# Scaling and DMA transposes of each batch placed in the order of their loads, in a retention-plus-MLP kernel

## The chip, the cores and the metric

The kernel runs on one core of a Trainium2 chip. The metric is the device time of one execution in microseconds (us). The record marks a run as slow when it lies over 1.5% above the fastest of its kernel.

The engines in the views: PE is TensorE (matmul), PEld its weight loads, DVE is VectorE, ACT ScalarE, POOL GpSimd, SP SyncE. A "q" behind an engine (SPq, ACTq) is its queue, in which it issues DMAs.

## The reference

Eight batches of eight heads, 576 tokens of width 64, go through a retention layer; the result (4608 tokens of width 512) goes through an MLP with a Swish whose slope is an input. All is float32 in memory.

```python
scores = scale * np.matmul(q, k.transpose(0, 1, 3, 2))
ret = scores * Dmat[None]                    # gamma_h ** (i - j) where i >= j, else 0
x = np.matmul(ret, v)                        # then heads side by side: [4608, 512]
h = x @ w_in                                 # [4608, 2048]
g = h / (1.0 + np.exp(-beta * h))
return g @ w_out                             # [4608, 512]
```

## The kernel before

The kernel is one long, hand-ordered program. TensorE's bulk is the MLP, cut into *fill steps* of four 512-column matmuls; block m computes the MLP of batch m while the attention of the next batch is slipped between its steps. All other work hangs on a number: the fill step before which it is put into the program of its engine. Each engine works strictly in that order.

```python
def merged(fill, *streams):
    todo = sorted((x for st in streams for x in st), key=lambda x: x[0])
    for n, f in enumerate(fill):
        while todo and todo[0][0] <= n:
            todo.pop(0)[1]()
        f()
```

A batch of attention is four chunks of 128 tokens; each pair of batches has a *tail* for the 64 tokens left over of both. A chunk needs these stages, each on another engine:

```python
# load_q, load_kv, load_tail: SyncE issues the loads
# pre_q(b, n), pre(i):        POOL scales queries and values, casts keys to bf16
# x_q, x_k, x_tail:           ScalarE issues a DMA that transposes
# a_sc, a_O, a_st:            TensorE: scores, output, state
def turn(dst, src):
    nc.scalar.dma_start_transpose(dst.rearrange("p j pr s -> p (j pr) s"), src.rearrange("p j h d -> p (j h d)"))
```

The distances between these stages are the numbers in question. Chunk `(b, c)` is computed at step `at`:

```python
def group(i, at):
    ...
    if b is None:                                              # a tail
        st += [(at - 27, F(load_tail, c)), (at - 15, F(pre, i)), (at - 10, F(x_tail, i))]
    else:
        near = b == 2
        if c == 0:
            xs, ps = ((10, 8), (15, 14, 13, 12)) if near else ((13.5, 12), (19, 18, 17, 16))
            st += [(at - 31, F(load_q, b))] + [(at - a, F(pre_q, b, x)) for x, a in enumerate(ps)]
            st += [(at - a, F(x_q, b, x)) for x, a in enumerate(xs)]
        if c % 2 == 0:                                         # keys and values, by pairs of chunks
            p0, p1, x0 = (9, 8.5, 5) if near else (15, 14.5, 10.5)
            st += [(at - 28, F(load_kv, n)), (at - 27.5, F(load_kv, n + 1)), (at - p0, F(pre, i)),
                   (at - p1, F(pre, i + 1)), (at - x0, F(x_k, b, c // 2))]
```

Batches 0 and 1 are transposed on TensorE instead, with a copy on ScalarE or VectorE behind it.

## Time and profile before

| | us |
|---|---|
| time, median of 3 runs at first | 326.29 |
| the same beside the changed kernel, 4 runs | 326.19 (325.56 to 327.77) |
| span of the profiled execution | 324.1 |
| TensorE busy | 303.4 (94%) |
| PE waits for transposed keys | 8.9 in two waits |
| batch 3's first scores start at | 96.79 |

The span and the busy times by engine are the head of the profile's page:

```profile
span 324.1 us, 5208 instructions
...
PE 303.4 (94%) x2078; PEld 153.2 (47%) x2113; DVE 109.7 (34%) x191; ACT 135.1 (42%) x236; POOL 103.8 (32%) x132
```

A share of 94% leaves about 20 us in which PE isn't busy, and some busy time that is stretched by a low clock. The share doesn't say which of these 20 us can be won. That takes the slices, the waits of PE and the chain of waits, which the prediction shows and reads.

### The profile page before, as it was taken

How to read it: one execution, taken by the hardware profiler on the slowest of the kernel's cores; microseconds unless marked ns; L12 is line 12 of the kernel's file. 1: busy time of each engine (PE TensorE's matmuls, PEld its weight loads, DVE VectorE, ACT ScalarE, POOL GpSimd, SP SyncE). 2: the span in 40 equal slices, each digit the busy share in tenths (PEclk: the TensorE clock that was granted, in tenths of full speed). 3: DMA queues.
4: the chain of work that ended last, by engine and by line, in shares of the span. 5: the costliest groups of instructions: out<-in, count | busy, mean ns of one | idle time of the engine just before them, and what ended most of it. 6: DMA issues, size and time to landing. Idle time of an engine off the chain costs nothing.

```text
span 324.1 us, 5208 instructions
## 1 busy us (share of the span) xinstructions
PE 303.4 (94%) x2078; PEld 153.2 (47%) x2113; DVE 109.7 (34%) x191; ACT 135.1 (42%) x236; POOL 103.8 (32%) x132
## 2 busy tenths in 40 slices
PE   6779989986499999999999999999999999999996
PEld 4544446432245444544454445444544544444444
DVE  6745665013245213522452246103622520020012
ACT  5567336560104740374027502750276107505800
POOL 2653785606820382138228210283310000000000
PEclk9799999999699999999999999999999999999999
DMA  8999999999916999499989643999711100022002
GB/s 203 242 359 386 369 215 265 194 266 236 220 68 172 206 213 189 133 207 198 243 227 197 106 122 99 224 212 221 185 39 32 62 37 32 2 66 65 2 38 92
DMA packets 127592, 53.83 MB, mean 166 GB/s; under 512 B 109888, under 2 KB 119504, under 8 KB 127568
## 3 DMA queue, kind: packets, MB, share of 16 engines
q1 hardware_dynamic: 97968, 46.15, 60.2%
q10 hardware_dynamic: 29600, 7.35, 14.2%
q8 instruction: 16, 0.26, 0.4%
q14 instruction: 8, 0.07, 0.1%
HBM read 36.71 MB, written 9.44 MB: 142 GB/s over the span
## 4 chain that ended last, share of the span: by engine, by line
PE 83%; DMA 8%; SPq 4%; issue 1%; DVE 1%; POOL 1%; ACT 0%
PE po L405 37%; PE ph L392 35%; PE O L350 3%; PE sc L312 3%; SPq L91 3%; DMA wt<-in_moe_w_in_dram 2%; DMA kvn<-in_v_dram 2%; PE O L336 2%; DMA qT<-qs 2%; PE st L375 2%; DMA kT<-kn 2%; SPq L80 1%; DVE ot L412 1%; PE O L333 0%; POOL kn L265 0%
## 5 line engine op out<-in xcount | busy, mean ns | idle before, releaser
L392 PE MATMUL ph<-xT,w_in_sb 128*128 128x512 bf16 (+2 forms) x577 | 127.4, 373 | 2.5 <-ACT w_in_sb L178 1.3
L405 PE MATMUL po<-w_out_sb,gT 128*128 128x512 bf16 (+2 forms) x588 | 127.9, 370 | 1.0
L394 ACT ACTIVATE gT<-ph,beta_sb 128x512 bf16<-128x512 f32 (+2 forms) x148 | 98.5, 675 | 62.0 <-PE ph L392 58.9
L392 PEld LDWEIGHTS <-w_in_sb 128*128 128x128 bf16 x592 | 56.4, 98 | 65.8 <-ACT w_in_sb L178 1.7
L405 PEld LDWEIGHTS <-gT 128*128 128x128 bf16 x608 | 57.6, 98 | 62.2 <-issue 1.4
L317 DVE TENSOR_TENSOR R<-sc,causal 128x512 bf16<-128x512 f32 x72 | 46.3, 684 | 82.8 <-PE sc L312 82.8
L412 DVE COPY ot<-po 128x512 f32<-128x512 f32 (+2 forms) x38 | 25.2, 663 | 113.5 <-PE po L405 112.3
L242 POOL TENSOR_TENSOR qs<-qn,gq 128x512 bf16<-128x512 f32 x26 | 27.0, 1061 | 62.9 <-DMA qn<-in_q_dram 48.9
L266 POOL TENSOR_TENSOR vn<-kvn,gv 128x512 bf16<-128x512 f32 x32 | 33.3, 1042 | 25.9 <-PE st L375 12.4
L380 ACT CAST sbd<-st 64x256 bf16<-64x256 f32 x48 | 17.6, 366 | 52.8 <-PE st L375 34.8
L265 POOL CAST kn<-kvn 128x512 bf16<-128x512 f32 x32 | 19.5, 609 | 22.5 <-DMA kT<-kn 7.1
L312 PE MATMUL sc<-qT,kT 64*128 64x128 bf16 x256 | 13.3, 224 | 10.0 <-DMA kT<-kn 8.9
L380 ACT CAST end<-st 64x256 bf16<-64x256 f32 x16 | 5.8, 365 | 37.4 <-PE st L375 37.3
L363 DVE CAST xT<-O 128x512 bf16<-128x512 f32 x29 | 19.7, 680 | 2.7 <-PE O L350 1.8
L312 PEld LDWEIGHTS <-kT 64*128 64x128 bf16 x288 | 8.4, 96 | 24.0 <-issue 11.4
L350 PE MATMUL O<-R,vn 128*64 128x128 bf16 x288 | 15.6, 230 | 0.0
L375 PE MATMUL st<-vn,kn 128*128 128x128 bf16 x128 | 12.9, 226 | 0.2 <-POOL vn L266 0.2
L350 PEld LDWEIGHTS <-vn 128*64 128x64 bf16 x288 | 9.6, 112 | 4.3 <-issue 0.8
L336 PE MATMUL O<-qT,sbd 128*128 128x128 bf16 x96 | 9.9, 228 | 0.0
L192 POOL TENSOR_SCALAR w_out_sb<-wt,rbeta_sb 128x512 bf16<-128x512 f32 x4 | 8.4, 2093 | 3.7 <-DMA wt<-in_moe_w_out_dram 3.7
L375 PEld LDWEIGHTS <-kn 128*128 128x128 bf16 x128 | 8.7, 101 | 1.2 <-issue 0.2
L192 DVE TENSOR_SCALAR w_out_sb<-wt,rbeta_sb 128x512 bf16<-128x512 f32 x12 | 6.8, 624 | 4.2 <-DMA wt<-in_moe_w_out_dram 4.2
(55 smaller groups left out, 78.3 us busy)
## 6 DMA issues: line engine op xcount, KB each, us to landing
qn<-in_q_dram SPq DMA_DIRECT2D x16, 512.0 KB, 5.6
kvn<-in_k_dram SPq DMA_DIRECT2D x32, 256.0 KB, 5.7
kvn<-in_v_dram SPq DMA_DIRECT2D x32, 256.0 KB, 5.3
out_dram<-ot SPq DMA_DIRECT2D x31, 256.0 KB, 2.7
wt<-in_moe_w_out_dram SPq DMA_DIRECT2D x4, 1024.0 KB, 9.2
wt<-in_moe_w_in_dram SPq DMA_DIRECT2D x3, 1024.0 KB, 10.2
out_dram<-ot SPq DMA_DIRECT2D x9, 128.0 KB, 2.3
wt<-in_moe_w_in_dram SPq DMA_DIRECT2D x2, 512.0 KB, 6.5
```

The source lines that it names most:

```text
L242: e.tensor_tensor(batch[b]["qs"][:, cs, hs], q_tiles[b][:, hs, cs].rearrange("p h i d -> p i h d"), gq[:, cs, hs].unsqueeze(3).to_broadcas ...
L266: nc.gpsimd.tensor_tensor(vn[:], t[:, 1], gains(gv, c), ALU.mult)
L312: nc.tensor.matmul(view(sc[j][:, p, :]), L["kT"][r, p, :], rhs, start=True, stop=True, skip_group_check=True)
L317: nc.vector.tensor_tensor(R[:, j], sc[j][:], m_b, ALU.mult)
L350: nc.tensor.matmul(O[j * D:(j + 1) * D, p, :], vn[:, 2 * p + j, :], R[:, j, p, :], start=p == 0 and not (early and crossed), stop=early or ...
L363: (nc.scalar.copy if i < E and i != CB - 1 else nc.vector.tensor_copy)(x, O[:])
L375: nc.tensor.matmul(st[:, p, :], heads(L["kn"], p), heads(L["vn"], p), start=(c == 0 and p == 0), stop=True, skip_group_check=True)
L380: nc.scalar.copy(s[r, :, j * D:(j + 1) * D], st[r, :, j * D:(j + 1) * D])
L392: nc.tensor.matmul(ph, w_in_sb[:, ko, fo * P:(fo + 1) * P], xts[m][:, ko, :, w], start=(ko == 0), stop=(ko == KO - 1))
L394: nc.scalar.activation(gts[m][:, fo, :, w], ph, ACT.Silu, scale=beta_sb[:, fo:fo + 1])
L405: nc.tensor.matmul(po[:, :nn], gT[:, fo, ms, :], w_out_sb[:, fo, n0:n0 + nn], start=(fo == 0), stop=(fo == FO - 1))
L412: nc.vector.tensor_copy(ot, po[:, :nn])
```

## The change

The intent is that each engine meets its work in the order in which the data arrive. Scaling and transposes of a chunk come in the order of their loads, loads of the later batches are issued later (fewer buffers wait full), and the first piece of the input weights is three columns of blocks wide, so that TensorE can do three steps before it needs the second.

```diff
-    pieces = [(0, 256), (256, 256)] + ...
+    pieces = [(0, 384), (384, 128)] + ...
 # cast_w_in: one more cast on ScalarE
-            if g == 1 and ko < 2:
+            if g == 1 and ko < 2 or g == 0 and ko == 0:
 # cast_w_out: a quarter of the scaling goes from POOL to ScalarE
-            e = nc.gpsimd if i == KO - 1 else nc.vector
-            e.tensor_scalar(w_out_sb[:, fo, :], t[:, i], rbeta_sb[:, fo:fo + 1], None, ALU.mult)
+            if i == KO - 1:
+                nc.scalar.activation(w_out_sb[:, fo, :], t[:, i], ACT.Copy, scale=rbeta_sb[:, fo:fo + 1])
+            else:
+                nc.vector.tensor_scalar(w_out_sb[:, fo, :], t[:, i], rbeta_sb[:, fo:fo + 1], None, ALU.mult)
 ... # batch 0's fourth chunk: O half a step later; batch 1's groups: key transpose beside its scores
-    steps(4, d0 + 7.5, d0 + 9.5, d0 + 10.5, d0 + 11, d0 + 11.5, d0 + 11.8),
+    steps(4, d0 + 7.5, d0 + 9.9, d0 + 10.7, d0 + 11.5, d0 + 11.6, d0 + 11.9),
 ... # group(i, at)
-                st += [(at - 27, F(load_tail, c)), (at - 15, F(pre, i)), (at - 10, F(x_tail, i))]
+                st += [(at - 24, F(load_tail, c)), (at - 12, F(pre, i)), (at - 8, F(x_tail, i))]
-                    xs, ps = ((10, 8), (15, 14, 13, 12)) if near else ((13.5, 12), (19, 18, 17, 16))
-                    st += [(at - 31, F(load_q, b))] + ...
+                    xs, ps = ((8.5, 7), (14, 13, 12, 11)) if near else ((11, 9.5), (17, 16, 15, 14))
+                    st += [(at - 24, F(load_q, b))] + ...
-                    p0, p1, x0 = (9, 8.5, 5) if near else (15, 14.5, 10.5)
-                    st += [(at - 28, F(load_kv, n)), (at - 27.5, F(load_kv, n + 1)), ...
+                    p0, p1, x0 = (13, 12, 8.5) if c else (9, 8.5, 5.5) if near else (13, 12, 7.5)
+                    st += [(at - 23, F(load_kv, n)), (at - 22.5, F(load_kv, n + 1)), ...
```

More of the change, by code (lines that the diff above doesn't have):

```diff
@@ L157 @@
     WG = 4
-    pieces = [(0, 256), (256, 256)] + [(f, 512) for f in range(512, d_ff, 512)]
+    pieces = [(0, 384), (384, 128)] + [(f, 512) for f in range(512, d_ff, 512)]
     NP = len(pieces)
@@ L489, in steps @@
         return list(zip(at, (F(pre, i), F(t_k, i), F(a_sc, i), F(a_st, i), F(a_cross, i, True), F(a_O, i))))
-    streams = [steps(3, 0, 1, 2, 3, 3, 3),
-               [(0.1, F(load_w_out, 0)), (2, F(cast_w_in, 1)), (6, F(cast_w_in, 2)), (6.2, F(load_w_out, 1)),
+    streams = [steps(3, 0, 1, 2, 3.5, 3.5, 3.5),
+               [(0.1, F(load_w_out, 0)), (2.5, F(cast_w_in, 1)), (6, F(cast_w_in, 2)), (6.2, F(load_w_out, 1)),
                 (10, F(cast_w_in, 3)), (10.1, F(load_w_out, 2)), (14, F(cast_w_in, 4)), (14.1, F(load_w_out, 3))],
@@ L495 @@
                [(14.2, F(load_q, 1))] + [(14.2, F(load_kv, n)) for n in range(CB, E)],
-               [(d0 + 7, F(pre_q, 1, n)) for n in range(4)] + [(d0 + 8.5, F(t_q, 1, 0)), (d0 + 9.5, F(t_q, 1, 1))],
-               steps(4, d0 + 7.5, d0 + 9.5, d0 + 10.5, d0 + 11, d0 + 11.5, d0 + 11.8),
-               steps(5, d0 + 9, d0 + 10.7, d0 + 11.6, d0 + 12, d0 + 12.5, d0 + 12.8),
-               steps(6, d0 + 10, d0 + 11.9, d0 + 12.7, d0 + 13, d0 + 13.5, d0 + 13.8),
-               steps(7, d0 + 11, d0 + 12.9, d0 + 13.7, d0 + 14, d0 + 14.5, d0 + 14.8)]
+               [(d0 + 7, F(pre_q, 1, n)) for n in range(4)] + [(d0 + 8.5, F(t_q, 1, 0)), (d0 + 9.8, F(t_q, 1, 1))],
+               steps(4, d0 + 7.5, d0 + 9.9, d0 + 10.7, d0 + 11.5, d0 + 11.6, d0 + 11.9),
+               steps(5, d0 + 9, d0 + 11.2, d0 + 11.8, d0 + 12.5, d0 + 12.6, d0 + 12.9),
+               steps(6, d0 + 10, d0 + 12.2, d0 + 12.8, d0 + 13.5, d0 + 13.6, d0 + 13.9),
+               steps(7, d0 + 11, d0 + 13.2, d0 + 13.8, d0 + 14.5, d0 + 14.6, d0 + 14.9)]
     def group(i, at):
@@ L513, in group @@
                 if c == 0:
-                    xs, ps = ((10, 8), (15, 14, 13, 12)) if near else ((13.5, 12), (19, 18, 17, 16))
-                    st += [(at - 31, F(load_q, b))] + [(at - a, F(pre_q, b, x)) for x, a in enumerate(ps)]
+                    xs, ps = ((8.5, 7), (14, 13, 12, 11)) if near else ((11, 9.5), (17, 16, 15, 14))
+                    st += [(at - 24, F(load_q, b))] + [(at - a, F(pre_q, b, x)) for x, a in enumerate(ps)]
                     st += [(at - a, F(x_q, b, x)) for x, a in enumerate(xs)]
                 if c % 2 == 0:
-                    p0, p1, x0 = (9, 8.5, 5) if near else (15, 14.5, 10.5)
-                    st += [(at - 28, F(load_kv, n)), (at - 27.5, F(load_kv, n + 1)), (at - p0, F(pre, i)),
+                    p0, p1, x0 = (13, 12, 8.5) if c else (9, 8.5, 5.5) if near else (13, 12, 7.5)
+                    st += [(at - 23, F(load_kv, n)), (at - 22.5, F(load_kv, n + 1)), (at - p0, F(pre, i)),
                            (at - p1, F(pre, i + 1)), (at - x0, F(x_k, b, c // 2))]
```

## The prediction

> **What bounds the kernel now.** I read the page's slices first, because a kernel whose TensorE is 94% busy can only gain where it is not.
>
> ```profile
> PE   6779989986499999999999999999999999999996
> ...
> PEclk9799999999699999999999999999999999999999
> DMA  8999999999916999499989643999711100022002
> ```
>
> A slice is 8.1 us. TensorE (PE) is short of work in the first three slices, in slices 9 to 11 (about 73 to 97 us), and in the last. The clock dips with it in slice 11. The DMA engines are full from the start to 90 us. After 97 us PE has no hole until the end, so the change can win only before that. Two-microsecond windows show the hole (columns: busy of PE, PEld, DVE, ACT, POOL, then granted clock, DMA share, GB/s):
>
> ```profile
> 80.00:82.00 2.00, 0.00 (x0) 0.00 (x0) 0.00 (x0) 0.00 (x0) 2.00 (x3) 1.00 1.04 226
> ...
> 84.00:86.00 2.00, 0.57 (x10) 0.38 (x12) 0.00 (x0) 0.57 (x2) 2.00 (x3) 0.50 1.31 251
> 86.00:88.00 2.00, 2.00 (x20) 1.50 (x19) 1.89 (x3) 0.38 (x2) 0.53 (x2) 0.50 0.97 215
> 88.00:90.00 2.00, 2.00 (x6) 0.70 (x5) 0.00 (x0) 0.35 (x1) 1.86 (x3) 0.59 1.12 251
> ```
>
> PE idles while POOL works without pause; after the idle time PE runs at half clock until about 90 us. PE's waits say for what:
>
> ```profile
> PE sc L312 <- DMA kT<-kn: 8.9, 2, 7.3
> ...
> PE ph L392 <- ACT w_in_sb L178: 1.3, 1, 1.3
> ```
>
> Two waits for transposed keys make 8.9 us: 7.3 (78.1 to 85.4 us) and 1.6 (67.3 to 68.8 us). The chain that ended last shows how the longer one came about (start, duration, what):
>
> ```profile
> 60.44 7.02 DMA qT<-qs
> ...
> 67.48 0.39 SPq L80
> ...
> 69.50 7.45 DMA kvn<-in_v_dram
> ...
> 76.97 0.70 POOL qs L242
> ...
> 77.95 0.61 POOL kn L265
> ...
> 79.51 0.61 POOL kn L265
> ...
> 80.15 5.23 DMA kT<-kn
> ...
> 85.42 0.61 PE sc L312 x8
> ```
>
> POOL scales batch 3's q (L242) before it casts the keys of batch 2's chunks 2 and 3 (L265, 77.95 and 79.51). Batch 3's q was issued at 67.48 and POOL could start on it at 75.97 only (the timeline). The key loads of chunks 2 and 3 had been issued at 56.5 to 61.0, so their casts stood about ten microseconds behind a load they have nothing to do with. That is order on POOL, not work.
>
> The cost of the hole: 8.9 us idle. At low clock the four attention steps after it took 0.61, 0.64, 0.61, 0.63 us in the timeline, against 0.40, 0.41, 0.39, 0.40 warm (0.9 us more), and 10 output matmuls took 3.25 us where 16 take 3.45 in the chain at 93.3 (1.1 us more); the next five lost 0.2. Together 2.2 us. So hole and clock cost 11.1 us, and their complete removal would give 326.3 - 11.1 = 315.2 us.
>
> One more thing shapes the DMA order. The compiled program gives all its DMAs eight completion semaphores in turn, so a DMA waits for the eighth before it. SyncE's waits show loads standing behind transposes with which they share no data:
>
> ```profile
> SPq L91 <- DMA qT<-qs: 13.8, 3, 5.4
> ```
>
> **What the Trainium skill says.** "DMA: Bandwidth & Descriptors", Queues, rings and completion order: each DMA engine takes its queue rows in turn, packet by packet. The trace agrees: with loads and transposes both queued, three transposes (queries 58.7 and 60.4, keys 63.05 us) were complete only at 68.7, and a query transpose took 7.0 us against a median of 5.0. "TensorE: Matmul & The Clock Gate", Why this matters for your kernels: idle gaps beyond some 3 us cost the clock. Here the clock was still 1.00 in 80 to 82 and 0.70 in 82 to 84, some 4 us into the gap; the 1.6 us gap cost none. "GPSIMD Engine Reference", Specifications: POOL shares its SBUF interface with VectorE in some modes. It fits the weight scaling on POOL, 2.09 us each beside VectorE's, where a POOL cast of equal shape takes 0.61.
>
> **The change, part by part.** A position in the lists is a fill step: four 512-column matmuls, 4 x 0.216 = 0.86 us (16 in 3.45). An attention group is 0.33 + 0.34 + 0.33 + 0.33 = 1.33 us.
>
> *Order on POOL.* Chunks 2 and 3 of batch 2 are at steps 56.5 and 60.75. Their casts move from 47.5 and 48, between batch 3's query scalings (46 to 49), to 43.5 and 44.5, before all of them (48 to 51). Their transpose moves from 51.5 to 48. This removes the 7.3 us wait and its 2.2 us of clock, 9.5 us, if nothing else comes late.
>
> *Order of loads.* SyncE isn't paced by steps, only by buffers, shared semaphores and stores whose data is not ready. So a later position moves a load only past a store or a transpose. Before 60 us the one effect is that batch 0's first three stores go ahead of batch 2's chunk loads 2 and 3: 0.75 MB at about 370 GB/s, 2 us. In later batches the tail's loads come ahead of the queries', and some loads after one or two stores; the transposes have lead to spare there.
>
> *First wait.* The query transposes of batch 2 move from 38 and 40 to 39.5 and 41: behind two more activations on ACT for the first (1.7 us), one more for the second. The key transpose stays behind step 42. The three then start at about 60.5 instead of 58.7 and share the engines with loads that the stores have pushed back. They needed 10 us before; I expect them done at 69.5 to 70.5, and a first wait of 2.3 to 3.0 us instead of 1.6. Loss about 1 us.
>
> *Batch 3.* PE reaches batch 3's first chunk at 96.79 now. From 68.84 to there without hole it is 17 steps (14.7 us) and three groups and a bit (4.2 us): 87.7, or 88.7 to 89.2 with the longer first wait. Are its data there? The DMA engines are full, so I count what they must move. Before, they emptied at 90 us, having done all this and batch 3's third chunk's keys and values (0.5 MB) and one store (0.25 MB); without these, at 220 GB/s, 87 us. By the chain: chunk 3's keys land about 71, queries of batch 3 about 78, four POOL scalings of 1.04 to 82.4, two casts to 84.6, a transpose of 4 to 5.3 us: 88.6 to 90. So PE gets to this point at about 89.5: 7.3 us earlier than 96.79. After it I see no new stall: lead of the key transposes falls from 10.5 to 7.5 or 8.5 steps, 6.5 us or more with a group in it, against a median landing of 5.4, and before the first chunk of most batches ACT has no activations to hold them back.
>
> *Weight pieces.* Three columns of blocks can be computed from the first piece, so the 1.3 us wait at L392 moves one step later. But the last quarter's matmuls need batch 0's chunk 3, whose O now comes after the fourth step: VectorE's 0.70 us copy, so far hidden beside a step, is exposed. The piece is 256 KB larger and lands up to 0.8 us later, and POOL's next cast with it. In sum -0.2 to +0.6 us.
>
> *Weight scaling on ACT.* Four of 2.09 us leave POOL (8.4 us) and become four of about 0.69 (the activation of equal shape) on ACT, idle from 35.8 to 43.3. Off the path; it gives POOL about 0.5 us at 43.
>
> *Batch 1's groups.* Each key transpose on PE moves next to the scores that use it. ACT's copy, 0.58 us and some latency, had a whole step to hide in; now one or two attention steps of 0.33. Three times 0.2 to 0.4: about +0.7 us.
>
> Sum for what lies before batch 3: the last two losses only move PE's arrival, which is then about as late as its data (89.5 to 90), so part of them is absorbed. 326.3 - 7.5 = 318.8 us.
>
> **Rivals.** (1) The hole goes entirely: transposes land as PE arrives and the first wait shrinks as well. For it: the full DMA engines also ran at only 180 to 200 GB/s in 76 to 80 us, which better order could win back. It would give 315 to 316. (2) The hole moves: the engines stay full until 87 to 90, and the wait for keys is put off to batch 3's first chunk, with another clock drop. For it: DMA share about 1 all along, and POOL and ACT take their work in order. Against it: 0.75 MB less to move by then. It would give 321 to 323. (3) A wait of the shared semaphores blocks SyncE somewhere new, or a shorter lead stalls a later batch. Nothing in the leads says so; a stall of 3 us with a clock drop in one batch would cost about 4 us: 323. (4) The start loses: all of it at most 1.5 us.
>
> **Range and chances.** Arrival at batch 3 between 86.5 and 92.5, with everything after unchanged, gives 316 to 322. A gain of 2% is 6.5 us, just below my 7.5, and my uncertainty is some 2.5 us: faster 0.62, within 2% 0.36, slower 0.02.
>
> **What would show it.** Right: the two waits for kT fall from 8.9 to between 2 and 5 us in total, none above 3.5; no slice after the start with a clock below 9; POOL's casts for batch 2 before batch 3's queries and their end near 72; scores of batch 3's first chunk near 89.5; PE's w_in_sb wait below 1 us. Wrong: a wait over 4 us anywhere, DMA still full beyond 92 us, or a new wait in batches 4 to 7, where I expect none.

## The result

| | before | after |
|---|---|---|
| time, median of 4 runs, us | 326.19 (325.56 to 327.77) | 322.59 (321.66 to 323.76) |
| span of the profile, us | 324.1 | 321.0 |
| batch 3's first scores at, us | 96.79 | 89.06 |
| from there to the end, us | 227.3 | 231.9 |

The ratio is 0.9884, with a 95% interval of 0.9836 to 0.9932: 1.2% faster by this ratio, which counts as the same within 2%. A ratio here is the mean time of one kernel's fast runs over the mean of the other's in the same rounds, so it isn't quite the ratio of the two medians. The prediction was 318.8 in a range of 316 to 322. The result lies 0.6 us outside the range and in the less likely class.

The table already says where the prediction went wrong. Up to batch 3's first scores the change wins 7.7 us, more than its whole gain. After that point, where I expected no difference, it loses 4.6.

**What went as intended.** These are PE's waits in the changed kernel (what waited for what: us in total, times, longest):

```profile
PE sc L314 <- DMA out_dram<-ot: 2.6, 1, 2.6
PE sc L314 <- ACT kT L297: 1.8, 5, 0.7
...
PE ph L394 <- ACT gT L396: 1.2, 2, 0.9
...
PE ph L394 <- DVE xT L365: 0.8, 1, 0.8
...
PE sc L314 <- DMA kT<-kn: 0.2, 1, 0.2
```

Under the name `kT<-kn` 0.2 us of the 8.9 are left (the first line, 2.6 us, turns out below to be a wait for keys too). POOL's timeline shows why (start, duration, what, idle time before it and what ended that):

```profile
63.32 0.61 POOL L267 CAST kn<-kvn 128x512 bf16<-128x512 f32 x1 [1.45 <-DMA kvn<-in_k_dram]
...
65.58 0.61 POOL L267 CAST kn<-kvn 128x512 bf16<-128x512 f32 x1
...
75.33 4.05 POOL L244 TENSOR_TENSOR qs<-qn,gq 128x512 bf16<-128x512 f32 x4 [5.32 <-DMA qn<-in_q_dram]
```

The two casts that stood at 77.95 and 79.51 behind batch 3's queries now start at 63.32 and 65.58. The first waits for its own load; the second follows without idle time. The queries, at 75.33, hold up nothing of batch 2. The 2 us windows, in the columns that the prediction names, answer to those from before:

```profile
84.00:86.00 2.00, 2.00 (x29) 1.33 (x29) 1.50 (x4) 0.51 (x2) 0.79 (x2) 1.00 1.32 254
86.00:88.00 2.00, 2.00 (x11) 0.88 (x9) 0.40 (x1) 0.22 (x1) 1.04 (x1) 1.00 1.22 319
```

PE is busy without a pause there and its clock is 1.00, where it was 0.50.

**What was given back.** In the list of waits the first line is new: 2.6 us, once. The slices say when (40 of 8.0 us):

```profile
PE   7879988989999999999999999999799999999996
...
PEclk9599999999999999999999999999799999999999
DMA  8999999999959879996998919969731110032012
```

Slice 28, at 224 to 232 us, has a 7 for PE and a 7 for the clock in a stretch that was all 9 before. (The 5 in the clock's second slice is the start; the mean clock of the first 24 us was 0.86 here, 0.93 before and 0.79 in pool_order_only, which has the old start.) The chain of waits of this stretch (start, duration, what):

```profile
221.62 2.60 PE po L407 x12
...
224.25 0.70 DVE ot L414
...
224.97 1.89 DMA out_dram<-ot
226.86 0.39 PE sc L314 x8
227.25 0.51 PE O L352 x8
227.75 0.54 PE O L335 x8
228.30 6.43 PE ph L394 x24
```

PE is through with the matmuls before at 224.22 and begins the scores of batch 7's first chunk at 226.85. The chain names a store as what ended the wait, but the scores read nothing that a store writes. A releaser is what came last by the profile, and two things came at nearly the same moment. The answer is in the waits of the weight load for the same scores, and in the view of the tile kT for 205 to 232 us:

```profile
PEld L314 <- DMA kT<-kn: 3.1, 1, 3.1
```

```profile
DMA to landing us min/median/max: 6.5/7.0/7.5
```

ScalarE issued the transpose of these keys at 219.27. It is the longer of the two in that view, 7.5 us, so the keys were there at about 226.8. So PE waited for keys, and the store landed beside them.

After the idle time the clock dropped, to 0.50 in one 2 us window:

```profile
228.00:230.00 2.00, 2.00 (x11) 0.84 (x9) 1.17 (x2) 0.00 (x0) 0.21 (x1) 0.50 0.90 196
```

The three attention steps took 0.39, 0.51 and 0.54 us where the same forms take 0.33 to 0.34 warm, 0.4 us more. The following 24 up-projection matmuls took 6.43 us in this chain instead of 24 x 0.216 = 5.18, 1.25 more. With the wait of 2.64 this makes 4.3 of the 4.6 us that were given back.

**Why the keys were late.** ScalarE's queue before, at the same place in the program (start, duration of the issue):

```profile
215.71 1.25 ACTq L272 DMA_TRANSPOSE qT<-qs  x1
216.99 1.93 ACTq L272 DMA_TRANSPOSE kT<-kn  x1
220.48 1.25 ACTq L272 DMA_TRANSPOSE qT<-qs  x1
221.85 1.95 ACTq L272 DMA_TRANSPOSE kT<-kn  x1
```

and after:

```profile
212.82 1.83 ACTq L274 DMA_TRANSPOSE kT<-kn  x1
214.76 4.39 ACTq L274 DMA_TRANSPOSE qT<-qs  x2
219.27 2.29 ACTq L274 DMA_TRANSPOSE kT<-kn  x1
```

The keys of the first chunk are the last line of each. Before, they were issued at 221.85 for scores at 231.81: 10.0 us ahead. After, at 219.27 for a PE that was ready at 224.22: 4.95 us ahead. In this stretch ScalarE has no activations, so the fill steps don't pace it. It runs from one item to the next, and the last thing that holds it up is a copy of the state, which it can make when PE has done the group at step 183.3. Before, two of the four transposes stood ahead of that copy. Now all four stand behind it and are issued in a row, and the last of them begins 6.45 us after the first. POOL had the keys ready at 214.6.

A second thing changed at the same time. SyncE's queue in the changed kernel:

```profile
212.15 0.36 SPq L417 DMA_DIRECT2D out_dram<-ot  x1
212.61 0.55 SPq L91 DMA_DIRECT2D kvn<-in_k_dram  x1
...
215.63 2.32 SPq L91 DMA_DIRECT2D kvn<-in_v_dram  x1
```

The loads of batch 7's second pair (1 MB) stand behind batch 5's first store now and run in the same microseconds as the transposes. That is only in part new: before, these loads were issued from 213.01 to 221.80, ahead of the store at 223.33, and also ran beside transposes; batch 7's keys then landed in 5.8 us, with 10.0 us of lead. So there are two suspects: transposes that start later, and loads beside them that slow them down.

### The profile page after: what moved, and what is told of

The parts are those of the page before. It is cut to its first block, busy times and chain, and to the rows that moved or that the text cites.

```text
span 321.0 us, 5240 instructions
## 1 busy us (share of the span) xinstructions
PE 306.6 (96%) x2113; PEld 153.6 (48%) x2113; DVE 108.3 (34%) x191; ACT 138.0 (43%) x241; POOL 96.2 (30%) x127
## 4 chain that ended last, share of the span: by engine, by line
PE 81%; DMA 10%; POOL 3%; SPq 3%; issue 1%; ACT 1%; DVE 1%; POOLq 0%; DVEq 0%
PE po L407 35%; PE ph L394 35%; PE O L352 3%; PE sc L314 3%; SPq L91 2%; DMA kT<-kn 2%; DMA wt<-in_moe_w_in_dram 2%; DMA qT<-qs 2%; DMA qn<-in_q_dram 2%; PE st L377 2%; PE O L338 2%; POOL qs L244 1%; DMA kvn<-in_k_dram 1%; DMA out_dram<-ot 1%; ACT kT L297 1%
## 5 line engine op out<-in xcount | busy, mean ns | idle before, releaser
L394 PE MATMUL ph<-xT,w_in_sb 128*128 128x512 bf16 (+2 forms) x592 | 129.8, 376 | 3.2 <-ACT gT L396 1.2
L407 PE MATMUL po<-w_out_sb,gT 128*128 128x512 bf16 (+2 forms) x608 | 129.5, 368 | 0.0
L204 PE MATMUL ph<-warm 128*128 128x256 f32 (+1 forms) x16 | 6.1, 533 | 1.3 <-DVE warm L113 1.3
L194 DVE TENSOR_SCALAR w_out_sb<-wt,rbeta_sb 128x512 bf16<-128x512 f32 x12 | 5.1, 482 | 5.5 <-DMA wt<-in_moe_w_out_dram 5.5
```

The lines of the kernel that those rows point to most:

```text
L394: nc.tensor.matmul(ph, w_in_sb[:, ko, fo * P:(fo + 1) * P], xts[m][:, ko, :, w], start=(ko == 0), stop=(ko == KO - 1))
L407: nc.tensor.matmul(po[:, :nn], gT[:, fo, ms, :], w_out_sb[:, fo, n0:n0 + nn], start=(fo == 0), stop=(fo == FO - 1))
```

## The experiments

The theory to test: the change is worth its 7.5 us, and the stall at batch 7 gave 4.3 of them back. A rival: the changed kernel loses the time in other parts (weight pieces, batch 1's groups, scaling on ScalarE), and the stall is only where slack shows. Inside the theory the two suspects have to be told apart. All eight kernels gave correct results. All runs are fast but one of turns_groups_old, 322.88 us, 1.6% above that kernel's fastest; its clock, 0.989, is no lower than the others', so the mark may be only spread. The first four kernels ran in one and the other four in another chip. The kernel before had a median of 325.2 (323.56 to 327.93, 7 runs) beside the first four and 326.71 (325.54 to 328.33, 11 runs) beside the other four.

| kernel | median us (lowest to highest) | ratio to before, 95% |
|---|---|---|
| b7_all_old | 319.56 (319.15 to 320.50) | 0.9810, 0.9745 to 0.9876 |
| b7_loads_old | 318.89 (318.69 to 319.12) | 0.9794, 0.9739 to 0.9849 |
| b7_turns_old | 318.63 (318.53 to 318.88) | 0.9787, 0.9733 to 0.9842 |
| pool_order_only | 320.02 (318.63 to 321.44) | 0.9829, 0.9760 to 0.9898 |
| rest_only | 327.51 (327.04 to 328.27) | 1.0027, 1.0000 to 1.0054 |
| turns_groups_old, fast runs | 319.46 (317.90 to 322.54) | 0.9787, 0.9739 to 0.9835 |
| turns_start_groups_old | 320.87 (319.85 to 321.67) | 0.9821, 0.9790 to 0.9851 |
| turns_start_old | 319.59 (319.35 to 321.08) | 0.9796, 0.9756 to 0.9836 |

**b7_all_old.** The changed kernel, with all of batch 7's loads, scaling and transposes, and those of the two tails around it, at the positions of before:

```diff
+            if b == B - 1 or b is None and i > len(seq) - 8:
+                ...                                     # loads, scaling, transposes as in the kernel before
+            else:
+                ...                                     # as in the changed kernel
```

> The changed kernel, with batch 7 and the tail pair before it (loads, scalings, transposes) put back to their old positions. Both theories of the late stall expect it to go: PE's wait of 2.6 us at 224.2 us and the low clock until about 232 us vanish, worth 2.6 + 1.7 = 4.3 us: 322.6 - 4.3 = 318.3 us, a profile with no wait of PE over 1 us after 92 us. If the time stays above 321 us, the 4 us were lost somewhere else than at batch 7.

Measured: 319.56, 1.3 us above the expectation, span 318.8. PE's longest wait for keys is 1.73 us. The waits for `kT<-kn` are 2.6 us in two, the longer of 1.73 at batch 2 (71.61), the other 0.9 in batch 6 (203.55); batch 3's first scores come at 90.18, a microsecond later than in the changed kernel. From there to the end it takes 228.6 us, against 231.9 in the changed kernel. So the stall at batch 7 goes with batch 7's positions, and 3.3 of the 4.6 us that had been given back return.

**b7_loads_old.** Only the loads of batch 7's second pair five steps earlier, so that they are issued ahead of the store:

```diff
+                    lo = 5 if b == B - 1 and c else 0
-                    st += [(at - 23, F(load_kv, n)), (at - 22.5, F(load_kv, n + 1)), ...
+                    st += [(at - 23 - lo, F(load_kv, n)), (at - 22.5 - lo, F(load_kv, n + 1)), ...
```

> Only the loads of batch 7's second pair go back, ahead of batch 5's first store. Theory LOADS (these loads, now issued at 212.6 to 217.9 us, share the DMA engines with the four transposes issued from 212.8 us on and slow them): the two query transposes are issued in about 2.8 us as in batch 4 instead of 4.4, the first key transpose starts by 217.3 instead of 219.3 us and lands within 5.5 us instead of 7.5, so no wait: 318.3 us. Theory TURNS (the transposes stand too late in ACT's queue, behind the state copy of step 184): the wait stays above 1 us and the time above 320.5 us.

Measured: 318.89. The loads are issued from 206.42 on and the store follows them at 212.84. The transposes are issued in the same order as in the changed kernel, the keys at 218.21, and PE begins the scores at 224.83 without a wait, 6.6 us later. The DMA view of 210 to 230 us (issues: what, how many, median us to landing) for the changed kernel:

```profile
kT<-kn ACTq DMA_TRANSPOSE x2, 7.0
```

and for this one:

```profile
kT<-kn ACTq DMA_TRANSPOSE x3, 4.4
```

The third transpose of this median is a later one. One by one, the tail's transpose landed in 4.4 instead of 6.5 us and batch 7's keys in 3.9 instead of 7.5 without the loads beside them (those of queries in a median of 4.3 instead of 7.7). The issues got shorter too: the three ahead of the keys held ScalarE's queue for 4.5 instead of 6.2 us, so the lead grew from 4.95 to 6.6. Moving the loads alone is enough to remove the stall.

**b7_turns_old.** The loads stay as in the change; only the scaling and transposes of batch 7's queries and first pair, and of the tail beside it, go back:

```diff
-                st += [(at - 24, F(load_tail, c)), (at - 12, F(pre, i)), (at - 8, F(x_tail, i))]
+                pt, xt_ = (15, 10) if c == 2 else (12, 8)
+                st += [(at - 24, F(load_tail, c)), (at - pt, F(pre, i)), (at - xt_, F(x_tail, i))]
...
+                    if b == B - 1:
+                        xs, ps = (13.5, 12), (19, 18, 17, 16)
...
+                    if b == B - 1 and c == 0:
+                        p0, p1, x0 = 15, 14.5, 10.5
```

> Only the scalings and transposes of batch 7's first pair, its queries and the tail before it go back; all loads stay where the change put them. Theory TURNS: the first query transpose and the tail's leave ahead of the state copy of step 184, the key transpose starts by 216 us and is there in time: no wait, 318.3 us. Theory LOADS: the key transpose still takes 6.5 us or more to land beside the second pair's loads, but as it starts some 3 us earlier a wait of at most 1 us is left and the clock stays up: 318 to 319.5 us. The landing time of the key transpose tells the two apart here, not the total.

Measured: 318.63, the fastest median and the tightest of the eight. The keys are transposed beside the loads and land in 8.3 us, no faster than in the changed kernel (7.5). They are issued at 214.87 though, 4.4 us earlier, and PE begins the scores at 224.61 without a wait. The issue of the keys in b7_loads_old and then here:

```profile
218.21 2.02 ACTq L274 DMA_TRANSPOSE kT<-kn  x1
...
214.87 3.30 ACTq L274 DMA_TRANSPOSE kT<-kn  x1
```

From batch 3's first scores (89.52) to the end of the span (317.2) it takes 227.7 us, as before the change (227.3).

So both suspects are real, and neither makes the stall alone. The later turn shortened the lead; the loads took the landing up to 7.5 us, and 1.7 us more off the lead by slowing the issues. Undoing either is enough. Relative to the changed kernel's median this is worth 322.59 - 318.63 = 4.0 us, taken from different calls; within the first call the changed kernel was not run again.

**pool_order_only.** The reverse: the kernel before, with nothing changed but where the casts and the key transpose of batch 2's second pair stand:

```diff
-                    p0, p1, x0 = (9, 8.5, 5) if near else (15, 14.5, 10.5)
+                    p0, p1, x0 = (13, 12, 8.5) if near and c else (9, 8.5, 5) if near else (15, 14.5, 10.5)
```

> The kernel before, with nothing changed but the casts and the transpose of batch 2's second pair (13, 12 and 8.5 steps ahead instead of 9, 8.5 and 5). If POOL's order alone made the 7.3 us wait, it goes with its clock drop, and batch 3's first scores, at 96.79 us before, come at 87.7 us if their data are there and at 89.5 us if the DMA engines decide: a gain of 7.3 to 9.1 us, 317 to 319 us, with no new stall at batch 7. Rival: the full DMA engines only move the wait to batch 3's first chunk, with 3 us of it left: 321 us or more.

Measured: 320.02, above the 317 to 319 expected, as a median of 318.63, 318.78, 321.25 and 321.44, two pairs with nothing between them. In the profiled run (span 317.0) both waits for `kT<-kn` are gone and batch 3's first scores come at 89.68. This one line alone thus makes as much as the whole change did (0.9829 against 0.9884), and less, though within the intervals, than the kernels without the stall (0.9794 and 0.9787). What separates the two pairs I can't say: only one run has a profile. It has a new wait in PE, 1.7 us in two for the state that ScalarE copies.

**rest_only.** The kernel before with the other parts alone: the weight pieces and their cast, batch 0's fourth chunk, the scaling on ScalarE, batch 1's groups; five rounds. The edit is everything in the change that stands ahead of `group`, loads and transposes staying as they were.

> The kernel before with only the change's other parts: wide first weight piece with its casts, batch 0's chunk 3 after the fourth step, last weight scaling on ACT, new order of batch 1's groups; the later batches as before. My theory (these parts cost PE 1.4 us by the start of block 1's first step, as 58.15 against 56.73 us in the two profiles): that step starts at 57.9 to 58.3 us; of this the 7.3 us wait may absorb a part, as it hangs on loads: 326.2 to 327.5 us. Rival (run-to-run spread of the start, as pool_order_only's profile had that step at 58.00 us with the old start): 325 to 326 us, same as before.

Measured: a ratio of 1.0027, at best nothing and at worst 0.5% slower. PE's waits show the old hole in place, 6.0 us long instead of 7.3, and batch 3's first scores at 98.85:

```profile
PE sc L314 <- DMA kT<-kn: 6.9, 2, 6.0
```

Block 1's first step came at 60.01, not at the 57.9 to 58.3 expected; the clock of the first 24 us was 0.79 in this profile. So the other parts of the change leave the hole in place, shorter only because PE comes to it later, and bring no gain of their own that five rounds could see.

**turns_groups_old.** b7_turns_old with batch 1's groups back as before, to see whether their loss of 0.9 us of waits comes back in the time; five rounds:

```diff
-               steps(4, d0 + 7.5, d0 + 9.9, d0 + 10.7, d0 + 11.5, d0 + 11.6, d0 + 11.9),
+               steps(4, d0 + 7.5, d0 + 9.5, d0 + 10.5, d0 + 11, d0 + 11.5, d0 + 11.8),
...                                                      # and chunks 5 to 7 likewise
```

> b7_turns_old with batch 1's groups in their old order. If the new order costs 0.8 us (three scores waiting for ACT's copy of the keys), block 1's first step starts at 57.3 to 57.5 us instead of 58.2 and the three waits for ACT's kT copy shrink from 1.8 us to about 0.9. The time: if batch 3's data decide when its first scores run (about 89 us), at most 0.5 us is left of it: 318.1 to 318.6 us; if PE's own work decides, 317.8 us.

Measured: 319.46 over the fast runs (320.07 with the slow one), above the expectation, with single runs from 317.90 to 322.54. PE's waits for the copied keys of batch 1 fall from 1.8 us (5 times) to 0.9 (2 times), as they should. But block 1 begins at 58.71, not at the 57.3 to 57.5 expected; the clock of the first 24 us was 0.79 again. Over the time nothing can be said: the fast runs spread over 4.6 us.

**turns_start_groups_old.** In addition the old weight pieces, their cast and batch 0's fourth chunk; five rounds:

```diff
-    pieces = [(0, 384), (384, 128)] + ...
+    pieces = [(0, 256), (256, 256)] + ...
-    streams = [steps(3, 0, 1, 2, 3.5, 3.5, 3.5),
+    streams = [steps(3, 0, 1, 2, 3, 3, 3),
...                                                      # and batch 1's groups as above
```

> b7_turns_old with the old start (two 256-wide pieces, chunk 3's O before the fourth step) and batch 1's old group order: what is left of the change is the order of the batches and the scaling on ACT. PE's own work decides: block 1's first step at 56.7 to 56.9 us, a gain of 1.4 us: 317.2 us. Batch 3's data decide at about 89 us: a gain of 0.5 us or less, 318.1 us, with the 1.4 us turned into waits before 90 us. The start's spread would show as a wider range of times than b7_turns_old's 318.53 to 318.88.

Measured: 320.87, where 317.2 or 318.1 was expected, and 2.2 us more than b7_turns_old had in its call; the kernel before was 1.5 us slower in this call, so by the ratios (0.9821 and 0.9787) the difference is 0.3%, and the intervals overlap. PE does begin block 1 earlier, at 56.70 instead of 58.20 us. Nothing comes of it: batch 3's first scores start at 92.19 instead of 89.52. PE's waits for 55 to 100 us show two waits for keys in place of none:

```profile
PE sc L314 <- DMA kT<-kn: 2.6, 2, 1.5
```

and SyncE's waits for 54 to 76 us what stood in the way:

```profile
SPq L91 <- DMA qT<-qs: 6.0, 1, 6.0
```

A load of values waits on a transpose of queries until 67.78 us. In the compiled program this load is the 46th DMA and has to wait for the 38th, whose semaphore it takes. Here the 38th is the transpose; in b7_turns_old it is a store, the transpose being the 39th, and the load goes out at 61.87. The edit has swapped two DMAs in the program's order, and that put a load behind a transpose. POOL begins batch 3's queries at 79.47 instead of 75.98. Their own load wasn't issued later for it (its second half at 69.30, against 69.8), but it landed after 10.0 us instead of 6.0. That the held load, now beside it, slowed it is likely and not shown.

**turns_start_old.** The old start with the new groups, three rounds: the last diff without its last line; the weight pieces' cast goes back with them.

> b7_turns_old with the old start alone. The last quarter of block 0's first steps starts at about 23.4 us instead of 24.1 where the clock is as in before's profile, block 1's first step at 57.5; time 318.0 to 318.6. Rival: the old start is the one that varies from run to run (24.7 us in pool_order_only's profile): then times spread by over 1 us and the median is no better than 318.6.

Measured: 319.59, above the 318.0 to 318.6 expected. The last quarter of block 0's first steps starts at 24.00, not at 23.4. The runs spread over 1.7 us, as the rival said; but turns_groups_old, with the new start, spreads wider. The profile has the same load held until 67.82 us, POOL at batch 3's queries at 77.72, and a wait for keys of 1.5 us at 90.12. It stands between the two kernels beside it. The differences among these last three are near the spread of runs, so I rank none of them.

The best of the eight by median and by worst run is b7_turns_old: 318.63 us, 2.1% under the kernel before (with an interval that includes 2%). By ratio turns_groups_old is level with it.

## Why the prediction was wrong

**Order on POOL: right.** The 7.3 us wait and its clock drop are gone, and PE reaches batch 3's first scores at 89.06, where the prediction said 89.5. The DMA engines empty at about 91 us (their share is 0.50 in 90 to 92 us and 0.01 after), where it had worked out 87. pool_order_only shows that this part alone removes the hole.

**First wait: size about right, kind wrong.** I expected 2.3 to 3.0 us for batch 2's keys in place of 1.6. What came was 0.95 and 0.26 us of waiting for the activation: ScalarE was held by the issue of three transposes (61.87, 63.32 and 65.56, of 1.33, 2.06 and 1.97 us), so the product of the up-projection wasn't taken from its buffer. Batch 2's first scores came at 70.19 instead of 68.85. That this delay of 1.3 is near the 1 us that I charged is luck: block 1 began 1.4 us later (58.15 instead of 56.73), and 1.2 us of new waits stand in place of the 1.6.

**Weight pieces: loss larger than I gave.** I gave -0.2 to +0.6 us. The wait for `w_in_sb` fell from 1.34 to 0.86 us, and the exposed copy of 0.8 appeared. The last quarter of block 0's first steps came at 24.09 instead of 23.41: +0.68 in this pair of profiles, just above the range. The beginning varies from run to run with the clock of the first 24 us, so profiles of the same mean clock should be compared. At 0.93: 23.41 with the old start, 24.12 with the new (b7_all_old). At 0.86: 24.00 (turns_start_old) and 24.09. At 0.79: 24.68 (pool_order_only), and 25.55 and 25.95 (turns_groups_old, rest_only). So the loss was 0.1 to 1.3 us, not -0.2 to 0.6.

**Weight scaling on ScalarE: right.** Four activations of 0.71 us each (I said 0.69) that PE did not wait for. VectorE's share of that work fell from 624 to 482 ns each with POOL gone from its side, which I had not counted. That POOL had slowed it is likely and not tested; it wasn't on the path.

**Batch 1's groups: right.** Predicted +0.7 us; the wait for ScalarE's copy went from 0.9 to 1.8 us, and the experiment that put the groups back showed 0.9 again.

**The step that failed** is this one, in the prediction's words: "After it I see no new stall: lead of the key transposes falls from 10.5 to 7.5 or 8.5 steps, 6.5 us or more with a group in it, against a median landing of 5.4". It stands in the paragraph on batch 3. Both sides of that comparison were off for batch 7. The lead was taken from the positions, as if ScalarE issued each transpose at its step. Its queue is a row of work in which an issue of a transpose takes about 2 us here (1.83, 4.39 for two, 2.29), and four of them stood behind one copy; the lead was 4.95 us. The landing was taken as a median over the run, and it was 7.5 us where 1 MB of loads ran beside it. Rival (3) of the prediction says what follows, "a stall of 3 us with a clock drop in one batch would cost about 4 us: 323"; it was 4.3 us and 322.59. It was dismissed with the sentence "Nothing in the leads says so". Two of the prediction's own signs showed it: a slice with a clock below 9, and a new wait in batches 4 to 7.

Without that stall the sum held: predicted 318.8, and the two kernels with one side of it undone measured 318.89 and 318.63. The close agreement is partly luck: the kernel before had 325.2 beside them, not the 326.3 that the prediction starts from, so the gains by these medians are 6.3 and 6.6 us, not 7.5. Batch 3's first scores, at 89.75 and 89.52, agree with its 89.5 without that help. Both kernels are 2.1% below the kernel before by the ratio; their intervals reach up to 0.985, so even these don't establish a gain of over 2%.

**On the Trainium skill's sentence on idle gaps** ("TensorE: Matmul & The Clock Gate", Why this matters for your kernels; some 3 us): here a gap of 2.64 us was followed by a clock of 0.82, then 0.50, in the 2 us windows from 226 us on. The prediction had taken from the kernel before that 1.6 us cost nothing. A stall of 2.64 us wasn't free.

**What stays open.** Why pool_order_only has two pairs of times, why turns_groups_old spreads over 4.6 us, why batch 3's queries landed late in turns_start_groups_old, and whether the weight pieces and batch 1's groups cost anything in the time: rest_only's interval of 1.0000 to 1.0054 says at most half a per cent.

## What to carry to other kernels

When work is moved later, check the lead at each of its uses, not at the one that the change is about. Take the lead as the time from the issue that the engine's own row of work allows, and the landing as it is with the transfers that will then run beside it. If two moves each eat a part of the same slack, as a later turn and later loads did here, look for the place where both fall together.

## What the Trainium skill lacked or had wrong

- "DMA: Bandwidth & Descriptors", Rules for kernel authors, says that a transpose next to ordinary DMAs needs nothing. That is about correctness, and all outputs here were correct. For time it misses what it costs: batch 7's keys landed in 3.9 us without loads beside them (b7_loads_old), and in 7.5 us (changed kernel) and 8.3 us (b7_turns_old) with 1 MB of loads beside them.
- No page gives, as a time on this chip, how long a DMA transpose holds the queue of the engine that issues it; "DMA: Bandwidth & Descriptors" has only cycle counts of unnamed "previous generations". Here it was 1.25 us at the shortest and 4.39 us for two in a row while the DMA engines were full. On ScalarE this held up activations, so PE waited 0.95 us.
- "TensorE: Matmul & The Clock Gate", Why this matters for your kernels: the limit on gaps of some 3 us. A gap of 2.64 us was followed by a clock of 0.50 here, while one of 1.6 us cost none.
- "DMA: Bandwidth & Descriptors" has no word on the time that a compiled program can lose by sharing a few completion semaphores among its DMAs: here eight are dealt out in turn, and in one kernel a load waited 6.0 us for a transpose with which it shares no data.
